# Moving two early loads from ScalarE's queue to SyncE's, so that ScalarE loads its function table after three loads

## The chip, the cores and the metric

One core of a Trainium2 chip. The metric is the device time of one execution in microseconds, the lower the better. A profile is one more such execution, with its span counted from the first instruction; spans are some 1.8 us shorter than times.

## The reference, cut to what matters

Attention over 8 batches of 12 heads (448 rows, 64 columns each), with a softmax whose denominator has one more term, then a two-layer network with a rational activation on the 3584 x 768 result.

```python
def _attn_ref(q, k, v):
    scores = scale * np.matmul(q, k.transpose(0, 1, 3, 2))
    m = np.max(scores, axis=-1, keepdims=True)
    e = np.exp(scores - m)
    attn = e / (np.sum(e, axis=-1, keepdims=True) + np.exp(-m) + 1e-09)
    return np.matmul(attn, v)
def _moe_ref(x, w_in, w_out, a, b):
    h = x @ w_in
    ...                       # g = P(h) / Q(h), cubic over quadratic
    return g @ w_out
```

## The kernel before

A planner in Python orders all operations by estimated times and emits them, each engine's in one fixed order. Four heads of one batch are a "quad". The first quads take a quick way: all of k and half of q of quad 0 come as six small loads (112 KB: two heads, half their rows), k and q of quad 1 as four loads (224 KB), from ScalarE's and SyncE's queues; they arrive as float32 and are cast to float16. Nearly everything later comes through GpSimd's queue. The small loads land in tiles `h` and `c`, the quad-1 loads in `g`; all are borrowed from the later part of the kernel.

```python
        def load(dma, src, h0, nh, stage, jh, nj, lat, deps=()):
            eng = nc.scalar if dma == "ACT" else nc.sync
            ...                                     # one dma_start; lat is the plan's guess of the landing
        plan.add("c0", piece(0, 0, 0, 2, "ACT", 2.8))          # small k, first pair of heads, first half
        plan.add("c0", piece(1, 0, 0, 2, "SP", 2.65))          # small q
        plan.add("c0", piece(0, 0, 2, 2, "ACT", 3.0, "ACT"))   # small k, second half: ScalarE casts it
        piece(1, 1, 0, 2, "SP", 3.0)
        piece(0, 1, 0, 2, "ACT", 3.4)                          # small k, second pair, first half
        piece(0, 1, 2, 2, "SP", 3.4)                           # small k, second pair, second half
        for pr in range(2):                                    # quad 1
            for ti, (src, dst, dma) in enumerate(((k, kn, "ACT"), (q, qn, "SP"))):
                stage = quad1_stage(ti, pr)
                d = load(dma, src, 4 + 2 * pr, 2, stage, 0, J, 4.3 + 1.1 * pr)
                cast(1, ti, pr, 0, J, dst[1][:, 2 * pr:2 * pr + 2], stage, d)
    ...
    table = plan.add("head", Op("table", "ACT", 1.3, [], lambda:
        nc.scalar.preload_act_table_set("natural_log_exp_and_others")))
```

In the profile each of the two queues holds back its second quad-1 load: SyncE waits 0.6 us for the landing of its very first load (at 3.27 us) and issues the load at 3.29; ScalarE issues its own at 3.51, after its very first load has landed (3.4). Scores of quad 0 come in four passes of four matmuls, each followed by one exponential on ScalarE. I call these the first to fourth exponential; the fourth is where the wait for quad 1 ends up.

The softmax here doesn't subtract the row's maximum and nothing guards it: scores larger than these inputs give would overflow.

## Time and profile before

| | before |
|---|---|
| time, three runs | 430.43, 430.86, 431.06 us |
| span of the profiled run (its time 431.38 us) | 429.6 us |
| TensorE busy | 418.6 us |
| fourth exponential starts | 10.44 us |
| first matmul of the input weights | 25.24 us |
| first quad-1 load of k: issued, landed | 2.22, 8.32 us |

How to read it: TensorE is full from 25 us to the end, with small gaps. The start-up ahead of that is the only part that the change can touch. The prediction shows the lines.

### The profile page before, as it was taken

How to read it: one execution, taken by the hardware profiler on the slowest of the kernel's cores; microseconds unless marked ns; L12 is line 12 of the kernel's file. 1: busy time of each engine (PE TensorE's matmuls, PEld its weight loads, DVE VectorE, ACT ScalarE, POOL GpSimd, SP SyncE). 2: the span in 40 equal slices, each digit the busy share in tenths (PEclk: the TensorE clock that was granted, in tenths of full speed). 3: DMA queues.
4: the chain of work that ended last, by engine and by line, in shares of the span. 5: the costliest groups of instructions: out<-in, count | busy, mean ns of one | idle time of the engine just before them, and what ended most of it. 6: DMA issues, size and time to landing. Idle time of an engine off the chain costs nothing.

```text
span 429.6 us, 8854 instructions
## 1 busy us (share of the span) xinstructions
PE 418.6 (97%) x3680; PEld 218.7 (51%) x3680; DVE 340.8 (79%) x513; ACT 328.0 (76%) x383; POOL 111.8 (26%) x174
## 2 busy tenths in 40 slices
PE   4999999999999999999999999999999999999996
PEld 2666664444444444455444445444444455555663
DVE  4437999999989998569987489984999999979500
ACT  4898999988999999744999984878878865585421
POOL 6455743543635103412206102320000100100000
PEclk9999999999999999999999999999999999999999
DMA  9999999999959742886338627914010101211222
GB/s 198 203 202 197 177 184 183 188 161 170 130 87 117 84 81 58 108 144 121 75 47 132 84 53 126 143 37 81 3 37 2 38 0 38 73 33 42 75 73 76
DMA packets 80297, 43.58 MB, mean 101 GB/s; under 512 B 36224, under 2 KB 76672, under 8 KB 80256
## 3 DMA queue, kind: packets, MB, share of 16 engines
q0 software_dynamic: 39040, 21.89, 39.0%
q1 hardware_dynamic: 39952, 20.26, 24.6%
q10 hardware_dynamic: 1264, 0.85, 0.7%
q8 instruction: 29, 0.48, 0.4%
q14 instruction: 12, 0.10, 0.1%
HBM read 45.62 MB, written 11.01 MB: 132 GB/s over the span
## 4 chain that ended last, share of the span: by engine, by line
PE 81%; DVE 14%; ACT 2%; DMA 1%; issue 1%; ACTq 0%; DVEq 0%
PE gen L718 33%; PE gen L620 29%; PE gen L554 11%; PE sps L519 8%; DVE h L637 3%; DVE n L661 2%; DVE n L657 2%; DVE c L661 1%; DMA g<-in_k_dram 1%; DVE g L661 1%; ACT e L527 1%; DVE x L582 1%; DVE c L657 1%; DVE w L657 1%; PE gen L435 1%
## 5 line engine op out<-in xcount | busy, mean ns | idle before, releaser
L527 ACT ACTIVATE e<-sps 112x896 f16<-112x896 f32 x192 | 167.4, 922 | 25.8 <-PE sps L519 25.0
L620 PE MATMUL gen<-x,w_in 128*128 128x448 f16 (+1 forms) x864 | 161.4, 332 | 0.4 <-DVE x L582 0.4
L718 PE MATMUL gen<-w_out,g 128*128 128x384 f16 (+2 forms) x768 | 134.8, 326 | 0.0
L620 PEld LDWEIGHTS <-w_in 128*128 128x128 f16 x864 | 79.6, 98 | 71.0 <-issue 17.7
L718 PEld LDWEIGHTS <-g 128*128 128x128 f16 x768 | 73.3, 98 | 56.2 <-issue 7.1
L637 DVE CAST h<-gen 128x448 f16<-128x448 f32 x113 | 68.8, 616 | 18.5 <-PE gen L620 18.1
L661 DVE TENSOR_TENSOR n<-n,h 128x1792 f16<-128x1792 f16 x64 | 70.1, 1096 | 0.9
L672 ACT ACTIVATE c<-c,oneeps_c 128x1792 f16<-128x1792 f16 x32 | 57.5, 1795 | 16.5 <-DVE c L661 16.4
L740 ACT ACTIVATE o<-gen 128x384 f32<-128x384 f32 (+2 forms) x56 | 27.6, 492 | 44.4 <-PE gen L718 44.2
L519 PE MATMUL sps<-qt,kt 64*128 64x448 f16 (+1 forms) x432 | 58.2, 342 | 2.3 <-ACT e L527 1.1
L675 ACT ACTIVATE c<-c 128x1792 f16<-128x1792 f16 x32 | 54.7, 1708 | 0.3
L695 POOL COPY gx<-g 128x1024 f16<-128x1024 f16 x8 | 9.4, 1173 | 155.1 <-DVE g L661 155.1
L582 DVE TENSOR_TENSOR x<-gen,lden 128x448 f16<-128x448 f32 (+1 forms) x54 | 28.2, 561 | 21.1 <-ACT lden L570 18.5
L657 DVE TENSOR_SCALAR n<-n,abc 128x1792 f16<-128x1792 f16 x64 | 44.1, 688 | 1.0
L554 PE MATMUL gen<-e,vn 112*32 112x448 f16 (+1 forms) x864 | 41.8, 337 | 0.0
L661 DVE TENSOR_TENSOR g<-n,c 128x1792 f16<-128x1792 f16 x32 | 35.3, 1102 | 7.0 <-ACT c L675 6.0
L661 DVE TENSOR_TENSOR c<-c,w 128x1792 f16<-128x1792 f16 x32 | 34.7, 1086 | 0.1
L519 PEld LDWEIGHTS <-kt 64*128 64x128 f16 x432 | 14.9, 96 | 36.7 <-issue 32.8
L318 POOL DMA_DIRECT2D vn<-in_v_dram x24 | 17.2, 719 | 61.8 <-PE sps L519 40.7
L480 POOL COPY kp<-kn 112x256 uint32<-112x256 uint32 x36 | 20.6, 602 | 39.8 <-DMA kt<-kp 37.0
L554 PEld LDWEIGHTS <-vn 112*32 112x32 f16 x864 | 23.1, 99 | 14.0
L657 DVE TENSOR_SCALAR n<-h,abc 128x1792 f16<-128x1792 f16 x32 | 25.3, 790 | 0.3
(45 smaller groups left out, 252.5 us busy)
## 6 DMA issues: line engine op xcount, KB each, us to landing
vn<-in_v_dram POOLq DMA_DIRECT2D x24, 224.0 KB, 7.4
kn<-in_k_dram POOLq DMA_DIRECT2D x22, 224.0 KB, 7.6
qn<-in_q_dram POOLq DMA_DIRECT2D x22, 224.0 KB, 8.0
w_in<-in_moe_w_in_dram POOLq DMA_DIRECT2D x12, 256.0 KB, 9.9
out_dram<-o SPq DMA_DIRECT2D x8, 336.0 KB, 3.2
out_dram<-o SPq DMA_DIRECT2D x8, 288.0 KB, 2.6
w_out<-in_moe_w_out_dram POOLq DMA_DIRECT2D x4, 512.0 KB, 14.9
out_dram<-o SPq DMA_DIRECT2D x7, 240.0 KB, 2.5
```

The costliest lines, as they stand in the source:

```text
L519: nc.tensor.matmul(out=sps[m % NS][0:(P if i == 0 and j == 1 else 128), hh, ci * qw:(ci + 1) * qw], lhsT=kt[n % NK][r, c0:c0 + (P if i == ...
L527: nc.scalar.activation(out=e_sb[m % NE], in_=sps[m % NS][0:P, :, 0:S], func=AF.Exp, scale=scale)
L554: nc.tensor.matmul(out=gen[unit["bank"]][32 * h:32 * h + 32, 0:qw], lhsT=lhs(h, j), rhs=e_sb[m % NE][:, h % 2, c0:c0 + qw], start=(j == 0) ...
L582: mult.emit = lambda s=s, uu=uu: nc.vector.tensor_tensor(out=x_sb[b % NX][:, 2 * qd + s, q0:q0 + qw], in0=gen[uu["bank"]][:, 0:qw], in1=ld ...
L620: nc.tensor.matmul(out=gen[unit["bank"]][:, fi * qw:(fi + 1) * qw], lhsT=w_in_sb[wg][:, c // 2, c % 2, (fc % FG) * 128:(fc % FG + 1) * 128 ...
L637: nc.vector.tensor_copy(out=dst, in_=src)
L657: return lambda: nc.vector.tensor_scalar(out=out, in0=in0, scalar1=s1, scalar2=s2, op0=op0, **kw)
L661: return lambda: nc.vector.tensor_tensor(out=out, in0=in0, in1=in1, op=ALU.mult)
L672: lambda: nc.scalar.activation(out=c, in_=c, func=AF.Ln, bias=oneeps_c)))
L675: lambda: nc.scalar.activation(out=c, in_=c, func=AF.Exp, scale=-1.0)))
L718: nc.tensor.matmul(out=gen[unit["bank"]][:, 0:wd], lhsT=lhs, rhs=w_out_sb[f][:, fc % FG, cols], start=(fc == 0), stop=(fc == NFC - 1))
L740: nc.scalar.activation(out=o[:, cols], in_=gen[unit["bank"]][:, 0:wd], func=AF.Copy)
```

## The change

The intent: ScalarE should be free for its function table, and then for its cast and the exponentials, earlier. SyncE, which has nothing else to do then, issues all four quad-1 loads. The new guesses of the landings keep the plan's order.

```diff
-            for ti, (src, dst, dma) in enumerate(((k, kn, "ACT"), (q, qn, "SP"))):
+            for ti, (src, dst) in enumerate(((k, kn), (q, qn))):
                 stage = quad1_stage(ti, pr)
-                d = load(dma, src, 4 + 2 * pr, 2, stage, 0, J, 4.3 + 1.1 * pr)
+                d = load("SP", src, 4 + 2 * pr, 2, stage, 0, J, (4.3, 3.87, 4.54, 4.11)[2 * pr + ti])
```

## The prediction

> **What bounds the kernel now.** I read the page first, then the chain of waits of the first 25 us, then the timelines of ScalarE, VectorE and SyncE over the same stretch, then the busy time by stretch.
>
> ```profile
> PE 418.6 (97%) x3680; PEld 218.7 (51%) x3680; DVE 340.8 (79%) x513; ACT 328.0 (76%) x383; POOL 111.8 (26%) x174
> PE   4999999999999999999999999999999999999996
> ```
>
> TensorE is busy in 418.6 of 429.6 us. Only the first of the 40 slices (10.7 us each) and the last are not full. So the kernel is one long full stretch with a start-up ahead of it. The change touches nothing after the first loads: the comparison of the instruction orders shows TensorE, VectorE and GpSimd the same, and differences on ScalarE and SyncE only in their first ten instructions. It can therefore move the start-up alone, and its worth is at most a part of the roughly 8 us in which TensorE waits there. Chain of waits, first 25 us (start, length, what):
>
> ```profile
> 0.74 0.43 ACTq L361
> 1.20 0.48 ACTq L361
> 1.71 0.48 ACTq L361
> 2.22 6.10 DMA g<-in_k_dram
> 8.35 0.44 DVE kn L366
> 8.83 1.08 PE gen L435 x16
> 9.91 0.51 PE sps L519 x4
> 10.44 0.93 ACT e L527
> ```
>
> The reader is to see that the function table is not in this list. What holds the start is one transfer: the first quad-1 load of k, issued by ScalarE at 2.22 us and landed 6.10 us later, at 8.32. VectorE's cast of it, sixteen transposes, one score pass and the fourth exponential (10.44 us) hang on it. Timelines of ScalarE and of VectorE (start, length, engine, line; in brackets the idle time before it and its end):
>
> ```profile
> 0.74 1.45 ACTq L361 DMA_DIRECT2D h<-in_k_dram  x3
> 2.22 1.61 ACTq L361 DMA_DIRECT2D g<-in_k_dram  x2
> 3.86 1.28 ACT L777 ACT_TABLE_LOAD   x1 [3.86 <-DMA h<-in_k_dram]
> 5.16 0.42 ACT L367 ACTIVATE kn<-h 112x256 f16<-112x256 f32 x1
> 8.35 0.43 DVE L366 CAST kn<-g 112x512 f16<-112x512 f32 x1 [0.56 <-DMA g<-in_k_dram]
> 8.69 0.58 DVE L366 CAST qn<-g 112x512 f16<-112x512 f32 x1
> 10.26 0.42 DVE L366 CAST kn<-g 112x512 f16<-112x512 f32 x1
> 10.59 0.42 DVE L366 CAST qn<-g 112x512 f16<-112x512 f32 x1
> ```
>
> ScalarE's second quad-1 issue does not follow the first. It stands at 3.51[...]. The table load stands behind it, at 3.86, and ScalarE's cast of a k half behind the table, at 5.16. VectorE sat idle for 0.56 us before the cast at 8.35: work that reaches it earlier only lengthens that wait, unless the load lands earlier too.
>
> [...] one issue is 0.3 to 0.5 us here, and from 3 to 4 us the two hardware queues held 51% and 55% of the engines and moved 312 GB/s together. [...] no run yet shows one queue alone with this work.
>
> **The change part by part.**
>
> 1. Two issues leave ScalarE. The table goes from 3.86 to about 2.22 and ends at 3.50 (2.22 + 1.28). The half of k that ScalarE casts was issued at 1.20 and took 3.0 us to land, so it is there at 4.2: the cast goes from 5.16 to about 4.25, 0.9 us earlier. The table becomes free.
>
> 2. Not all of that 0.9 us comes through. In TensorE's order the transposes of this half come after the first score pass, which starts at 4.83 and lasts 0.56. They can start at 5.2 to 5.3, not at 5.62: 0.35 us. The next copies, casts, passes and exponentials move by about this: the third exponential from 8.44 to about 8.1, and VectorE reaches the quad-1 cast at about 7.4 instead of 7.8.
>
> 3. There it meets the wait for the load. SyncE now issues k, q, k, q of quad 1. The first k starts right behind SyncE's three small loads, at about 2.17, as early as on ScalarE. The first q moves from 2.17 to about 2.65. The second k waits for the same landing as before and stays near 3.5. The second q stands behind it and moves from 3.29 to about 3.9.
>
> 4. The landings. Before, the first q and the first k were served side by side on two queues and landed at 8.07 and 8.32 (issue plus 5.9 and 6.1). Now they are served one after the other, with the same bytes before them. If the pair is done at the same time, q lands at 8.0 to 8.3 and k the length of one load earlier. From the second pair before (9.8 and 10.0, so 1.7 us per 448 KB) I estimate 0.9 us for 224 KB: k at about 7.4.
>
> 5. So VectorE casts k at about 7.45 and q at about 8.2, where it did so at 8.69: 0.5 us earlier. The score pass stands behind q's transposes in TensorE's order, so the fourth exponential moves with q, from 10.44 to about 9.95. The upper limit, if q did not make anyone wait, is 0.85 us (cast of q right behind k at 7.85).
>
> 6. Second pair: k at about 9.2, q at 10.0 to 10.4. Their transposes stood at 11.89, behind a score pass that waits for ScalarE; 0.5 us earlier is 11.4. Cast of q from 10.4 ends at 10.8. This fits.
>
> 7. Does the 0.5 us reach the end? From 10.4 to 25 us the chain is ScalarE's exponentials and TensorE, from 25 to 37 TensorE (12.00 of 12.00 us busy), from 37 to 97 VectorE, then TensorE. No TensorE wait for a load is named from 10 to 25 us. The nearest loads are q of quad 3 (landed 19.6, transposed 20.55) and the first input weights (the third issued 12.16, landed 24.3, first matmul 25.24): 0.9 us of room each, so 0.5 us passes. I take off 0.05 for small losses.
>
> Sum: 430.86 - 0.45 = 430.4 us.
>
> **The rivals.** **One queue is slower.** With only SyncE's queue loaded, the 16 DMA engines may not keep the rate that two queues reached (296 GB/s from 5 to 6 us, 270 from 6 to 7)[...]. For it: the load's landing is the chain. Against it: from 6 to 7 us SyncE's queue alone already held 73% of the engines with 184 packets to 100 of ScalarE's. If q lands at 8.7 the gain is 0; at 9.2 the kernel is 0.4 to 0.5 us slower, about 431.3.
>
> **Hidden anyway.** The pair lands as before, k no earlier, the cast of k stays at 8.35, and the 0.9 us of the table ends as longer idle time on VectorE. For it: the 0.56 us of idle there. The time would be 430.8.
>
> **The table was the start.** If the table and ScalarE's cast had set the pace, 0.9 us would come off, and with k early 0.85 us at most: 430.0. Against it: the chain does not hold the table.
>
> **A later load takes the gain.** The weights arrive through a queue that is full from 9 us on (196 GB/s, same before and after), with 0.9 us of room; this cuts a large gain, not 0.5.
>
> **Range and chances.** The runs before spread over 0.63 us, as much as the whole effect. Gain of 0.85 us with a low run gives 429.7; a loss of 0.3 us gives 431.2. This holds the first, second and third rivals and a mild form of the slower queue. Two per cent is 8.6 us, the whole idle time of TensorE in the start-up, so faster or slower by that much is all but out.
>
> **What would show it right or wrong.** Step 1: table at 2.2, cast at 4.2 to 4.3. Step 2: third exponential at about 8.1. Step 4: the landing of the first k (7.4) and q (8.0 to 8.3), read as issue plus time to landing. Step 5: the fourth exponential at 9.9 to 10.0, and the chain no longer starting with a ScalarE issue. Step 7: the same shift at the first input matmul (25.24) and in the last stretch. If q lands after 8.7, the slower queue is true; if the shift is there at 10 us and gone at 25, a later load took it; if the order of transfers makes a later wait longer than 0.9 us, the time rises and the prediction is wrong.

430.86 - 0.45 = 430.4 us is the forecast. The landing that the second k waits for in step 3 is that of ScalarE's very first load of k (3.4 us); in the profile of the changed kernel SyncE waits 0.3 us for it. While the table load ran, only SyncE's and ScalarE's queues moved packets (35% and 38% of the engines from 3.86 to 5.14 us in the profile before, 54% and 43% from 2.22 to 3.50 in the changed one), so it is not seen to take anything from the loads. By what rule queues share the engines was not shown; that the pair would land one after the other on one queue (step 4) was the author's estimate.

## The result, and the profile after

Four runs of each: 430.98 us median with the change (430.68 to 431.64), 430.96 us before (430.43 to 431.41). A ratio is the mean time of one kernel's fast runs over that of the other's of the same rounds, so not quite the ratio of the medians. It was 1.0003, 95% interval 0.9986 to 1.0020: the same, within about 0.7 us either way.

The profile says something else: its span was 428.9 us against 429.6. The start of the timeline of ScalarE in the changed kernel:

```profile
2.22 1.28 ACT L777 ACT_TABLE_LOAD   x1 [2.22 <-issue]
4.30 0.42 ACT L367 ACTIVATE kn<-h 112x256 f16<-112x256 f32 x1 [0.81 <-DMA h<-in_k_dram]
8.67 0.92 ACT L527 ACTIVATE e<-sps 112x896 f16<-112x896 f32 x1 [1.08 <-PE sps L519]
```

The table moved from 3.86 to 2.22 us, and ScalarE's cast from 5.16 to 4.30, where it now waits for its own load. The third line is the third exponential. It should have moved earlier too; it moved later, from 8.44 to 8.67. VectorE's timeline tells why:

```profile
6.77 0.67 DVE L366 CAST kn<-h 112x256 f16<-112x256 f32 x2 [0.75 <-DMA h<-in_k_dram]
7.93 0.42 DVE L366 CAST kn<-g 112x512 f16<-112x512 f32 x1
8.48 0.43 DVE L366 CAST qn<-g 112x512 f16<-112x512 f32 x1
```

The casts of quad 1 (tile `g`) came earlier than before, 7.93 and 8.48 against 8.35 and 8.69, and the idle time in front of them is gone. But 0.75 us of idle stands in front of the last two small loads of k (tile `h`), which were cast at 6.26 before. The chain of waits over the first 12 us agrees; it now starts with ScalarE's last small load:

```profile
1.71 5.04 DMA h<-in_k_dram
6.77 0.30 DVE kn L366
...
8.08 0.56 PE sps L519 x4
8.63 0.92 PE gen L435 x14
9.55 0.50 PE sps L519 x4
...
10.08 0.93 ACT e L527
```

That load was issued at the same 1.71 us as before and took 5.0 us to land, not 4.1. Even so the fourth exponential came 0.36 us earlier (10.08 against 10.44), the first input matmul 0.54 us (24.70 against 25.24), and the last copy of the output 0.65 us (425.35 against 426.00). So there were two questions. Is the gain in this pair of profiles real, when the times of eight runs showed none? And is the late small load the price of the change, or an accident?

### The profile page after: what moved, and what is told of

Its sections match the earlier page's. It is cut to its first block, busy times and chain, and to the rows that moved or that the text cites. A ratio compares the mean times of both kernels' runs of the same rounds, so it can differ in the third digit from the quotient of the medians.

```text
span 428.9 us, 8854 instructions
## 1 busy us (share of the span) xinstructions
PE 418.1 (97%) x3680; PEld 218.5 (51%) x3680; DVE 340.1 (79%) x513; ACT 328.2 (77%) x383; POOL 113.1 (26%) x174
## 4 chain that ended last, share of the span: by engine, by line
PE 81%; DVE 14%; ACT 2%; DMA 1%; issue 1%; ACTq 0%; DVEq 0%
PE gen L718 33%; PE gen L620 29%; PE gen L554 11%; PE sps L519 8%; DVE h L637 3%; DVE n L661 2%; DVE n L657 2%; ACT e L527 2%; DVE c L661 1%; DVE g L661 1%; DMA h<-in_k_dram 1%; DVE x L582 1%; DVE c L657 1%; DVE w L657 1%; PE gen L435 1%
```

## The experiments

The labels in brackets are those of the runs. Theory A: the change gains what the prediction said, and scatter hid it. Theory B: the late small load takes the gain back.

### Noise, and the changed kernel again (before_again, after_again)

No edit: both kernels as they are, five rounds on one chip. (The series ran on different chips, each with its own runs of the kernel before.)

> The unchanged kernel, timed against itself, as the measure of noise. Ratio 1.000, with an interval that tells what five rounds can resolve; I expect about plus or minus 0.0008 (0.35 us). Its profile is a second draw of the start-up: if the landing of the first quad-1 k (8.32 us in the first profile) and of the last small k loads (5.57 and 5.81) are fixed by the program, they come within 0.1 us of that; if they vary from run to run by 0.3 us or more, one pair of profiles cannot show what the change does.

> The changed kernel again. Theory A (the change gains, and the four runs only hid it in noise): ratio 0.9987 to 0.9992, a gain of 0.35 to 0.55 us, and the first quad-1 pair lands at 7.4 to 7.7 and 8.0 to 8.5. Theory B (the gain in the one profile is luck: one queue makes the last small k loads land later, 6.45 and 6.75 us there against 5.57 and 5.81 before, and this new wait takes the gain): ratio 0.9997 to 1.0005, and the late landing of the small loads is there again, later than 6.2.

Measured: before_again 0.9994 (0.9982 to 1.0006), after_again 0.9987 (0.9974 to 1.0000). Medians 430.79 and 430.46 us, against 431.15 for eleven runs of the kernel before in the same series. The interval is wider than the expected 0.0008. The control also warns: the kernel before, run under a second name, came out 0.26 us (0.0006) faster than itself, within its interval, and the changed kernel is 0.3 us (0.0007) below that. What the second profile of the unchanged kernel showed on VectorE, with the same columns as above:

```profile
6.48 0.52 DVE L366 CAST kn<-h 112x256 f16<-112x256 f32 x2
8.05 0.43 DVE L366 CAST kn<-g 112x512 f16<-112x512 f32 x1 [0.23 <-DMA g<-in_k_dram]
```

In the very same program the quad-1 load landed 0.3 us earlier than in the first profile (8.05 against 8.35 at the cast), and the last small load 0.6 us later (issued 1.71, 4.75 us to land: 6.46, against 5.84). The fourth exponential moved by 0.42 us without any change, more than the 0.36 us between the first two profiles. A pair of profiles cannot decide on a change of this size. after_again has the ratio of theory A, and the late small load of theory B as well (6.96 us). Its profiled run was the slowest of its six, 431.71 us. Something besides the landings must move the time; it comes below.

### The table without the loads (after_two_tables, after_two_sets, table_between)

First, the changed kernel with the table loaded twice, to make ScalarE late again (the diffs here are cut to the lines that matter):

```diff
-        nc.scalar.preload_act_table_set("natural_log_exp_and_others")))
+        nc.scalar.preload_act_table_set("natural_log_exp_and_others") for _ in range(2)]))
```

> The changed kernel with the function table loaded twice in a row, so that ScalarE is free at about 4.8 us instead of 3.5 (5.14 in the kernel before), the loads being those of the changed kernel. If only the loads matter (the early table is slack ahead of a landing): ScalarE's cast of the k half starts at 4.8, its transposes 0 to 0.1 us later than in the changed kernel because the first score pass stands before them, and the time is that of the changed kernel within 0.1 us. If the table is what the change gains by: 0.3 to 0.5 us slower than the changed kernel, as slow as the kernel before.

This was a miss: the build kept one of the two equal loads, and the profile shows one table load, at 2.22 us. So it is another repeat of the changed kernel: 430.66 us, ratio 0.9986 (0.9974 to 0.9998). Second try, with two different tables:

```diff
+        nc.scalar.preload_act_table_set(n) for n in ("exp_and_others", "natural_log_exp_and_others")]))
```

> The changed kernel with two different function tables loaded one after the other (the earlier attempt named two loads of the same table, of which the build kept one, so it was a repeat of the changed kernel). ScalarE is then free at about 4.8 us, near the 5.14 of the kernel before, with the changed kernel's loads. If the early table is slack: its cast at 4.8, the first transposes behind it at 5.3 and not more than 0.1 us later than the changed kernel's, the time that of the changed kernel within 0.15 us. If the early table is the gain: slower by 0.3 to 0.5 us.

Its timeline of ScalarE:

```profile
2.22 2.57 ACT L777 ACT_TABLE_LOAD   x2 [2.22 <-issue]
4.80 0.42 ACT L367 ACTIVATE kn<-h 112x256 f16<-112x256 f32 x1
6.64 0.92 ACT L527 ACTIVATE e<-sps 112x896 f16<-112x896 f32 x1 [0.34 <-PE sps L519]
```

The cast started at 4.80 instead of 4.30, and the second exponential at 6.64, where the changed kernel has it at 6.67: nothing came of the half microsecond. The ratio was 0.9988 (0.9976 to 1.0001), that of the changed kernel. So 1.28 of the 1.64 us by which the table moved are slack. The rest is not tested here: ScalarE is free at 4.79 us, still 0.35 us before the 5.14 of the kernel before, and the second exponential keeps all of its gain over the 7.00 there. The changed loads with the table as late as before were not run.

Third, the table alone, with the loads left split. It stands between ScalarE's two quad-1 issues:

```diff
                 d = load(dma, src, 4 + 2 * pr, 2, stage, 0, J, 4.3 + 1.1 * pr)
+                if dma == "ACT" and pr == 0: plan.add("head", table)
```

(The definition of `table` moves up for this, and the plan counts it as 0 us, so that the order of the other engines stays.)

> The quad-1 loads stay split between ScalarE and SyncE as before; the table alone moves ahead, between ScalarE's two quad-1 issues, so it runs at about 2.7 to 4.0 us and ScalarE's cast starts at about 4.25. If the landing of the first k on ScalarE's queue (8.3 us) sets the start: the cast of it stays at 8.3 and VectorE's wait before it grows from 0.56 to about 0.9 us; the time is that of the kernel before within 0.1 us. If the table was the cost: 0.35 us faster than before. If ScalarE's second k load now waits for the table to end, it is issued at 4.0 instead of 3.5 and lands 0.3 to 0.5 us later, which has about 1 us of room.

```profile
2.73 1.28 ACT L776 ACT_TABLE_LOAD   x1 [2.73 <-issue]
3.33 0.32 ACTq L360 DMA_DIRECT2D g<-in_k_dram  x1
4.27 0.42 ACT L366 ACTIVATE kn<-h 112x256 f16<-112x256 f32 x1 [0.26 <-DMA h<-in_k_dram]
```

The second line shows ScalarE issuing a load while its table load still runs, so this table load (2.73 to 4.01 us) did not hold up the issue at 3.33, only the other way round (in the kernel before, the table started at 3.86, right behind the issue that began at 3.51). The cast came at 4.27, almost 0.9 us earlier than before, and still the fourth exponential started at 10.67, behind the load of k that landed at 8.5 (issued 2.22, 6.3 us). Ratio 0.9991 (0.9979 to 1.0003), next to 0.9994 for no change at all in the same series: no gain can be told, and by time alone the 0.35 us that the table might have been worth is not excluded. The profile speaks against it: the fourth exponential started 2.2 us after the landing of that load, as in the two profiles of the kernel before (2.1 and 2.0). VectorE's wait for that load was 0.38 us, not the 0.9 expected, because the small load was late here too (6.9 us).

### How much later ScalarE may be (before_two_tables)

The same edit with two tables, in the kernel before.

> The kernel before with two different tables: ScalarE's cast of the k half goes from 5.2 to about 6.45 us, 1.28 later. My reading of the start-up gives this cast a slack of some 0.3 to 0.9 us ahead of the quad-1 cast on VectorE (which landed at 8.05 to 8.5); so the fourth exponential and the time move by 0.4 to 0.8 us, not by 1.28 and not by 0. The span less the start of the fourth exponential should be 419.0 plus or minus 0.3, as in the six profiles so far.

```profile
3.92 2.57 ACT L777 ACT_TABLE_LOAD   x2 [3.92 <-DMA h<-in_k_dram]
6.50 0.42 ACT L367 ACTIVATE kn<-h 112x256 f16<-112x256 f32 x1
11.15 1.72 ACT L527 ACTIVATE e<-sps 112x896 f16<-112x896 f32 x2 [0.46 <-PE sps L519]
```

The cast went 1.3 us later, the fourth exponential to 11.15 (10.44 and 10.02 before), and the ratio was 1.0016 (1.0004 to 1.0029), 0.7 us more. So a table later than the loads did cost here: of 1.3 us about half came through, and the rest was slack, as expected. The kernel before stood close to the edge of that slack, and the change moved it well inside.

### Which queue the small loads share (small_on_scalar, small_on_sync, small_on_sync_again)

Theory C: quad-1 loads on SyncE's queue overtake the last small load on ScalarE's. To make it worse, the fourth of the k halves also goes to ScalarE; to take it away, both halves of the second pair go to SyncE, ahead of quad 1 in the same queue (and the guesses of landings are adjusted, so that the order of all other engines stays):

```diff
-        piece(0, 1, 0, 2, "ACT", 3.4)
-        piece(0, 1, 2, 2, "SP", 3.4)
+        piece(0, 1, 0, 2, "SP", 3.4)      # small_on_scalar: "ACT" and "ACT" instead
+        piece(0, 1, 2, 2, "SP", 2.97)
```

> The opposite: SyncE's third small load (second half of the second k pair) moves to ScalarE, so that ScalarE's queue holds four small loads and the quad-1 loads on SyncE's start 0.5 us earlier, at about 1.67. Theory C (overtaking): the last small load lands later, at 7.2 to 7.8, the quad-1 pair earlier (k 6.8 to 7.3, q 7.6 to 8.2), the third exponential moves to 9.2 or later and the time is 0.3 to 0.6 us above the changed kernel's. Theory D (slow engine): the last small load lands within 0.3 us of the changed kernel's 6.7 to 6.9 and the time is the same. The table starts at about 2.7 and ends at 4.0, before its cast can start, so it costs nothing in either.

> The changed kernel with ScalarE's third small load (first half of the second k pair) also issued by SyncE, so that all loads of k's second pair and of quad 1 stand in one queue in the order of their use. Theory C (in the changed kernel the quad-1 loads on SyncE's queue overtake the last small load on ScalarE's queue in some DMA engines, and this late landing, 6.7 to 6.9 us, is the new wait): the last small loads land at 5.7 to 6.2 us, the third exponential starts at about 8.0 to 8.3 instead of 8.6 to 9.1, the second quad-1 load (q) lands at 8.2 to 8.7, and the time is 0.1 to 0.4 us below the changed kernel's, or the same if q's landing then takes over. Theory D (the late landing is a slow DMA engine's, whatever the queue): the last small loads land at 6.5 to 6.9 again and the time is that of the changed kernel.

VectorE in small_on_scalar:

```profile
7.30 0.29 DVE L366 CAST kn<-h 112x256 f16<-112x256 f32 x1 [1.22 <-DMA h<-in_k_dram]
8.76 0.29 DVE L366 CAST kn<-h 112x256 f16<-112x256 f32 x1 [1.17 <-DMA h<-in_k_dram]
```

VectorE in small_on_sync:

```profile
5.93 0.48 DVE L366 CAST kn<-h 112x256 f16<-112x256 f32 x2
7.38 0.42 DVE L366 CAST kn<-g 112x512 f16<-112x512 f32 x1
7.75 0.58 DVE L366 CAST qn<-g 112x512 f16<-112x512 f32 x1
```

On ScalarE's queue behind each other, the last small load took 6.5 us and landed at 8.7, a microsecond later than I expected even under theory C; SyncE's k of quad 1, issued before it, had landed at 7.1. Median time 431.92 us, ratio 1.0017 (1.0005 to 1.0030). On SyncE's queue the two small loads landed by 6.0, without a wait on VectorE; the third exponential started at 8.11 and the fourth at 9.50, with no late load in the chain. Ratio 0.9985 (0.9972 to 0.9999). The two differ by 1.4 us in the median, for the same bytes. Theory C holds as far as this: moving the small loads to the other queue moved the last landing (8.7 against 6.0 us), and the time went with it (the 1.4 us); a slow DMA engine whatever the queue (theory D) is out. "Overtake" is to be read in bytes. In no profile did a load of these two queues land before one issued earlier (the first two, issued together, aside). But when the last small load of the first changed profile landed, at 6.74 us, SyncE's queue had moved 0.88 MB, and its own three small loads are 0.34 MB: half a megabyte of quad 1, issued later, had gone ahead. Still, the changed kernel is not worse off in this than the one before. The last small load landed at 5.8, 6.5, 6.9 and 7.1 us in four profiles with the loads split, and at 6.7, 7.0, 6.7, 6.5 and 6.0 in five with the change. The kernel before has a quad-1 load of q on SyncE's queue behind three small ones too. So the late small load of the first profile was an accident that both kernels share; theory B falls.

> The version with four small loads on SyncE once more, to see whether it beats the changed kernel (whose ratios were 0.9987, 0.9986, 0.9988 and 0.9984 in four series of five rounds). If a fourth exponential that starts at 9.5 instead of 9.7 to 10.5 us comes through with the 0.72 found in the profiles, its ratio is 0.9975 to 0.9985; if the spread of the clock's moment swamps it, it cannot be told from the changed kernel's. In its profile the last small k load should land before 6.1 us, as in the two profiles with this placement so far; later than 6.5 would show that the placement does not hold it.

Once more 0.9985 (0.9972 to 0.9997), 430.39 us, fourth exponential at 9.66. Over its eleven runs this version has a mean of 430.41 us, the changed kernel over 21 runs 430.66. That is within the scatter, so it cannot be told from the changed kernel, though it beats the kernel before in both series (which share nine of their runs of the kernel before).

### The changed kernel a last time, and TensorE's clock (after_third, after_warm, small_on_sync_warm)

The profiles disagreed with their landings in one place. small_on_sync had its fourth exponential 0.6 us ahead of the first profile of the changed kernel, and by 17 us this lead was gone. The timelines of TensorE show why. First two lines of eight transposes each, in the first profile of the changed kernel:

```profile
15.28 0.39 PE L435 MATMUL gen<-ident,kn 112*64 112x112 f16 x8
15.50 0.36 PE L435 MATMUL gen<-ident,qn 112*64 112x112 f16 x8
```

The same place of the program in small_on_sync:

```profile
15.06 0.59 PE L435 MATMUL gen<-ident,kn 112*64 112x112 f16 x8
15.44 0.59 PE L435 MATMUL gen<-ident,qn 112*64 112x112 f16 x8
```

Eight transposes follow each other after 0.22 us in one run and after 0.38 us in the other. The clock record of the trace has TensorE's clock go to full at 14.79 us in the first, at 17.02 in the second. (The page's row of the granted clock shows 9 from the start: it has no entry for the time before. What shows of the "half clock" in an expectation below is the pace of such transposes: eight follow each other after 0.37 to 0.38 us in small_on_sync before that moment, and after 0.19 to 0.22 us in the changed kernel behind it.) Over the 14 profiles that moment lies between 14.00 and 17.98 us, for the same program too: 14.79, 17.98, 15.59 and 14.99 in four profiles of the changed kernel, 16.07 and 15.30 in two of the kernel before. It is always 3.4 to 6.6 us after the fourth exponential plus 1.0 us. In the twelve profiles without fillers (see below) TensorE's first stretch of more than 3 us without a gap begins there (at 11.40 us in the profile before, at 11.05 in the changed one); the stretches ahead of it are 2.9 us at most. In the profile before, TensorE was busy for 6.1 of the 9 us from 3 to 12 us, and the clock did not change then.

| profile | fourth exponential | clock full | first input matmul | span |
|---|---|---|---|---|
| before | 10.44 | 16.07 | 25.24 | 429.6 |
| before_again | 10.02 | 15.30 | 24.82 | 429.2 |
| table_between | 10.67 | 17.03 | 25.69 | 429.5 |
| before_two_tables | 11.15 | 17.05 | 26.05 | 430.0 |
| changed | 10.08 | 14.79 | 24.70 | 428.9 |
| after_again | 10.50 | 17.98 | 25.84 | 429.8 |
| after_two_tables | 10.04 | 15.59 | 24.85 | 429.0 |
| after_two_sets | 9.77 | 16.17 | 24.80 | 428.7 |
| after_third | 9.74 | 14.99 | 24.55 | 428.4 |
| after_warm | 10.25 | 16.84 | 25.28 | 429.1 |
| small_on_scalar | 11.44 | 15.89 | 25.96 | 429.9 |
| small_on_sync | 9.50 | 17.02 | 24.86 | 428.8 |
| small_on_sync_again | 9.66 | 14.14 | 24.20 | 428.1 |
| small_on_sync_warm | 9.65 | 14.00 | 24.12 | 428.1 |

A least-squares fit over these rows gives: first input matmul = 13.51 + 0.72 x fourth exponential + 0.26 x clock full, and none of the 14 is off by more than 0.06 us. From there to the end of the span it is 403.8 to 404.4 us in every profile. So two things go with the time: the landings, through the fourth exponential, of which 0.72 comes through, and the moment of the clock, whose 4 us of scatter are worth 1.0 us (0.26 x 4). No profile shows the change acting on the second: the clock's moments of the two kernels overlap. Theory E, a conjecture, was that matmuls that nobody reads would bring the clock's moment forward (in the kernel with the change, and in small_on_sync):

```diff
+            def fill(n):
+                for _ in range(n):
+                    nc.tensor.matmul(out=sps[1][:, 0, 0:128], lhsT=ident, rhs=ident, start=True, stop=True)
+            plan.add("att", Op("fill", "PE", 0.0, [ident_op], lambda: fill(22), mode="t"))
+            for op, n in ((first[1], 3), (first[2], 3)):
+                op.emit = lambda was=op.emit, n=n: (was(), fill(n))
```

> The changed kernel once more, beside the two below. In 30 fast runs of the kernel before and 21 of the changed one so far the means differ by 0.39 us: ratio 0.9988 to 0.9993 expected if that is true, 1.000 if it is chance. In ten profiles the first input matmul starts at 13.56 + 0.72 x (start of the fourth exponential) + 0.26 x (time at which TensorE's clock record goes to full), within 0.05 us; this one should fit within 0.1.

> The changed kernel with 28 matmuls on the identity (128x128, into a score buffer that the next score pass overwrites) that nobody reads: 22 of them before the first transposes (1.4 to 3.8 us, TensorE idle there) and 3 in each of two later gaps. Theory E (TensorE runs the start-up at half clock until 14.8 to 18.0 us, at a moment that differs from run to run, and this scatter hides the change): the clock goes to full before 12 us, the attention matmuls at 12 to 15 us take half as long, the first input matmul starts 0.8 to 2 us earlier (23 to 24 us) and the time falls by 0.8 to 2 us, ratio 0.995 to 0.998. If the clock only answers to longer work, it goes to full at 14.8 to 18 as before and the time is the changed kernel's or up to 0.2 us longer, from the six fillers in the gaps.

> The same fillers in the version with four small loads on SyncE, whose fourth exponential starts at about 9.5 instead of 10.1 us. Both together, if theory E holds: 0.3 to 0.5 us below the version above, and the lowest time of all, ratio 0.994 to 0.997. If a later load takes over once the start is 1.5 us earlier (q of quad 3 landed at 19.6 us, the first input weights at 24.3 in the kernel before), TensorE shows a wait for that load and the time stays at that of the version above.

after_third: 430.49 us, ratio 0.9984 (0.9972 to 0.9996). Its chain of waits is the one that the prediction had drawn up, starting at the second load of SyncE:

```profile
2.67 5.45 DMA g<-in_q_dram
8.15 0.44 DVE qn L366
8.63 0.58 PE gen L435 x8
9.21 0.51 PE sps L519 x4
9.74 0.93 ACT e L527
```

The load of q landed at 8.12 us, and the fourth exponential came at 9.74. The fit as it stood before gives 24.47 us for the first input matmul, and 24.55 was measured.

The fillers did not do it. They ran in TensorE's idle time:

```profile
1.36 2.53 PE L833 MATMUL sps<-ident 128*128 128x128 f16 x22 [1.36 <-POOL ident masks.py:199]
```

But the clock went to full at 16.84 us in after_warm and at 14.00 in small_on_sync_warm: inside the spread without fillers (14.14 to 17.98), and 0.14 us below its lower end. With the fillers, TensorE in after_warm shows no gap from 1.36 to 6.59 us, 5.2 us in a row, and only gaps of 0.2 to 0.3 us from there to 10.76. That is as long as the 3.4 to 6.6 us after which the clock changed elsewhere, and it did not change. Ratios 0.9993 (0.9979 to 1.0007) and 0.9985 (0.9973 to 0.9997); the single times of after_warm scatter from 430.06 to 432.19. That a late clock goes with a late first input matmul is shown by the fit and by the pace of the transposes; no run set the clock's moment on purpose, and a remedy is not shown. Whether fillers in every gap up to 11 us would do it stays open.

### What the times add up to

Four series of the changed program: 1.0003 (first series, four runs of each), 0.9987, 0.9986 and 0.9984 (five rounds each; the middle two share their runs of the kernel before). Their mean is 0.9990, which is 0.43 us of 431.1. Taken over single runs: 40 of the kernel before have a mean of 431.11 us, 21 of the changed one 430.66. Single runs scatter by about 0.4 us (standard deviation), so the standard error of this difference is about 0.11 us, and by this count the gain is clear of chance. (The count takes runs on several chips as one sample.) It is a tenth of a per cent, far inside "same". The first series, with four runs of each, was too small to show it.

## Why the prediction was right

The range held (429.7 to 431.2; 430.98 us in the first series), and so did "the same within 2%". The number 430.4 did not come: the first series shows no gain, and over all series the changed kernel has a mean of 430.66 us. The gain in all series, 0.43 us, is close to the 0.45 foretold, but the steps below account for about a third of it, so that this closeness is in part luck. By its own steps:

- **Step 1** (table at 2.2, cast at 4.25): right, 2.22 and 4.30.
- **Step 2** (not all of the 0.9 us comes through; third exponential at 8.1): the first half held. The second exponential gained 0.33 us (7.00 to 6.67). The third was to come at 8.1. It did so in after_third (8.06); in the other four profiles with the changed loads it came at 8.38 to 9.12, mostly later than the 8.44 and 8.48 of the kernel before. The step took the landing of the small loads in one profile for a property of the program; it varies by more than a microsecond (5.8 to 7.1 us).
- **Step 3** (the issues): right. SyncE issued at 2.17, 2.67, 3.49 and 3.85.
- **Step 4** (k at about 7.4, q at 8.0 to 8.3): right. In the first profile 7.6 and 8.5 (2.17 + 5.4 and 2.67 + 5.8), in after_third 7.2 and 8.1.
- **Step 5** (fourth exponential from 10.44 to 9.95): the target was right, the start was not. Five profiles with the changed loads have 10.08, 10.50, 10.04, 9.77 and 9.74, mean 10.03. But 10.44 was one draw of the kernel before; the second had 10.02. Two against five leave a shift of 0.2 us (10.23 less 10.03), uncertain by about as much. The path was right in part: in three of the five the fourth exponential came 1.6 us after the landing of q, as the step has it; in after_again and after_two_sets 2.5 and 1.9 us after it, held by the late small load. In four of the five, the first profile among them, the chain still starts with a ScalarE issue, that of this small load. The step had said that it would not.
- **Step 6** (second pair: k at about 9.2, q at 10.0 to 10.4): right, 9.34 and 10.15 in the first profile.
- **Step 7** (all but 0.05 us of the shift reaches the end): no later load took it; in that it was right. Its gap was TensorE's clock, which I read from the page's row as full throughout. A shift of the fourth exponential comes through by 0.72.

Of the rivals, the slower queue did not show: one queue landed the pair as early as two had (q, the last, at 7.9 to 8.5 us in five profiles; with two queues k, the last, at 8.0 to 8.7 in four). "Hidden anyway" fell with the landing of the first k of quad 1, at 7.0 to 7.6 us in the changed kernel against 8.3 and 8.0. "The table was the start" is not borne out: it was to bring 0.9 us, the gain is 0.43, and in table_between the fourth exponential followed the load. But how the 0.43 us divides between the table and the loads is not shown by the times, and before_two_tables shows that a table later than the loads did cost (0.7 us). A new wait did appear in some profiles, for the small loads, but it is as frequent without the change. What stays open: the profiles' own shift of 0.2 us, times 0.72, is 0.15 us, less than the 0.43 us timed; with two profiles of the kernel before, this cannot be settled.

## What to carry to other kernels

When an engine's first work is late, follow the chain of waits before moving that work: of the 1.6 us by which the function table moved here, 1.3 us could be given back without a cost that the times show, and with the table moved alone the start still followed a load. Put loads that are needed in order into one queue in that order; here, when they were split over two, bytes of later loads were moved ahead of an earlier one (half a megabyte in the first changed profile). And take two or three profiles of the same program before reading a difference of 0.1% out of a pair: here landings and the moment of TensorE's clock moved single runs by more than the change did.
